# Three-block DMA transposes in a fused attention and feed-forward kernel, with one half batch turned by TensorE instead

## Chip, cores and metric

The kernel runs on one core of a Trainium2 chip. The metric is the device time of one execution in microseconds (us), given as the median of several executions. A profile is of one execution; its span is some 1.7 to 1.9 us shorter than the time of the same execution. All runs below are single-core, and all were classed as fast, with a granted TensorE clock of 0.99 to 1.00.

## What is computed

Windowed attention over 8 batches, 8 heads, 576 tokens and head size 64, then four matrix products over the 4608 tokens:

```python
def _attn_ref(q, k, v):                       # (8, 8, 576, 64) each
    scores = scale * np.matmul(q, k.transpose(0, 1, 3, 2))
    rel = pos[:, None] - pos[None, :]
    mask_plain = (rel >= 0) & (rel < 32)                         # heads 0 to 3
    mask_dil = (rel >= 0) & (rel < 128) & (rel % 4 == 0)         # heads 4 to 7
    # ... masked softmax ...
    return np.matmul(attn, v)

x = attn_out.transpose(0, 2, 1, 3).reshape(4608, 512)
out = (((x @ w1) * (x @ w2)) @ w3) @ w_out
```

The kernel forms w3 @ w_out once, so that each tile of 512 tokens needs 64 matmuls with w1 and w2 and 32 with the fused matrix.

## The kernel before

Attention is done in steps: for each batch b, first the dilated heads (`u = 1`), then the plain ones (`u = 0`), each in two halves `hf` of 288 tokens. A step ends with its normalised values in `xo`: 96 tokens on the partitions, and along the free dimension 2 pairs of heads, 3 blocks of 96 tokens, 2 heads, 64 channels. The feed-forward part needs channels on the partitions, in `XT` (four chunks of 128 channels, 4608 tokens), so every block of every pair is transposed. The dilated steps of batches 2 to 7 do it by DMA from SyncE, one DMA for each block and pair. All others use TensorE and a copy from PSUM.

```python
def to_channels(self, ps=ps_x, copy=None):
    if self.u and self.b > 1:
        for hp in range(2):
            for m in range(3):
                t0 = self.b * S + HALF * self.hf + 96 * m
                nc.sync.dma_start(
                    out=XT[:, 2 + hp, t0 : t0 + 96],
                    in_=self.xo[0:96, hp, 2 * m : 2 * m + 2, :].rearrange("p h d -> p (h d)"),
                    transpose=True,
                )
        return
    xv = ps[:, 0 : 2 * HALF].rearrange("p (h s t) -> p h s t", h=2, s=4)
    for hp in range(2):
        for m in range(3):
            # ... xo = 96 columns of xv
            nc.tensor.transpose(out=xo, in_=self.xo[0:96, hp, 2 * m : 2 * m + 2, :],
                                identity=ident[0:96, 0:96])
    # ... dst = the half's place in XT
    if copy is None:
        copy = nc.vector.tensor_copy if self.u == 0 and self.b > 1 else nc.scalar.copy
    copy(out=dst, in_=xv)
```

The phases of attention are spread between the matmuls of the feed-forward tiles; `after` is the room that a phase gets:

```python
# from segment(), for step i, with p1 the step before and p2 the one before that; tests on st left out
later(st.scores, after=1.0 if p2 is not None and p2.u == 0 else 1.6)
if p2 is not None and p2.u == 0:
    later(p2.to_channels)
    # ...
if p1 is not None:
    later(p1.values, after=1.6)
    if p1.u:
        behind(p1.to_channels)          # DMA: issued by SyncE once xo is there and its queue is free
    # ...
```

The consumer is the first feed-forward product, which takes chunks 2 and 3 (the dilated heads) first (shortened; from tile 1 on):

```python
for c in (2, 3, 0, 1):
    nc.tensor.matmul(out=ps, lhsT=w_sb[:, c, f * P : (f + 1) * P],
                     rhs=XT[:, c, t * TB : (t + 1) * TB], ...)
```

Token tile t ends at token 512(t+1), and batch b begins at token 576b. So tile 2 (to token 1535) needs the first of the three blocks (tokens 1440 to 1535) of batch 2's second half, and tile 3 needs 32 tokens of batch 3's second half. Tiles 4 to 7 need only the first half of their own batch, and tile 8 the rest of batch 7. "Landing" is used below for the time from the issue of a DMA to the arrival of its data.

The softmax here doesn't subtract the row's maximum and nothing guards it: scores larger than these inputs give would overflow.

Of the kernel before, what the change touches and what calls it, by code (L numbers as in the profile page):

```python
# [19 lines left out]
S = 576  # L20
D = 64
ROWS = 18
HALF = 288
# [13 lines left out]
def kernel(  # L37
# [11 lines left out]
    nc = tc.nc  # L49
# [34 lines left out]
    XT = const.tile([P, DCH, n_tok], BF16, name="XT")  # L84
# [171 lines left out]
    class Step:  # L256
        def __init__(self, n, b, u, hf):
            self.b, self.u, self.hf = b, u, hf
            self.et = ets[n % NET]
            self.xo = {}  # L260

        def score_matmuls(self, heads, bank_of, start):
# [101 lines left out]
            self.normalize(ov, self.xo.rearrange("p h j d -> p (h j) d"), 4, 3)()  # L364

        def to_channels(self, ps=ps_x, copy=None):
            if self.u and self.b > 1:
                for hp in range(2):
                    for m in range(3):
                        t0 = self.b * S + HALF * self.hf + 96 * m  # L370
                        nc.sync.dma_start(  # L371
                            out=XT[:, 2 + hp, t0 : t0 + 96],
                            in_=self.xo[0:96, hp, 2 * m : 2 * m + 2, :].rearrange("p h d -> p (h d)"),
                            transpose=True,
                        )
                return
            xv = ps[:, 0 : 2 * HALF].rearrange("p (h s t) -> p h s t", h=2, s=4)
            for hp in range(2):
                for m in range(3):
                    if self.u == 0:  # L380
                        xo = xv[:, hp, :, 24 * m : 24 * m + 24]
                    else:
                        xo = xv[:, hp].rearrange("p s t -> p (s t)")[:, 96 * m : 96 * m + 96]
                    nc.tensor.transpose(  # L384
                        out=xo,
                        in_=self.xo[0:96, hp, 2 * m : 2 * m + 2, :],
                        identity=ident[0:96, 0:96],
                    )
            dst = XT[:, 2 * self.u : 2 * self.u + 2, self.b * S : (self.b + 1) * S]
            if self.u == 0:  # L390
                t0 = 72 * self.hf
                dst = dst.rearrange("p h (s t) -> p h s t", s=4)[:, :, :, t0 : t0 + 72]
            else:
                t0 = HALF * self.hf
                dst = dst[:, :, t0 : t0 + HALF].rearrange("p h (s t) -> p h s t", s=4)
# [3 lines that stand above are left out]
# [19 lines left out]
    def later(f, *args, after=1.0):  # L418

        phases.append([lambda: f(*args)])  # L420
        room.append(after)

    def behind(f, *args):

        phases[-1].append(lambda: f(*args))
# [64 lines left out]
    def segment(lo, hi):  # L490

        for i in range(lo, hi + 2):
            st = steps[i] if i < hi else None
            p1 = steps[i - 1] if lo <= i - 1 < hi else None
            p2 = steps[i - 2] if lo <= i - 2 else None
            at, b = i % 4, i // 4
            more = 4 * (b + 1) < hi and st is not None
            if st is not None:
                later(st.scores, after=1.0 if p2 is not None and p2.u == 0 else 1.6)
            if p2 is not None and p2.u == 0:  # L500
                later(p2.to_channels)
                done_at[i - 2] = len(phases)
            if p1 is not None:
                later(p1.values, after=1.6)
                if p1.u:
                    behind(p1.to_channels)
            if st is not None:
                if at == 0:
                    behind(transpose_qk, b, 0, 1)
                if at == 1:  # L510
                    if more:
                        behind(transpose_qk, b + 1, 1, 0)
                if at == 2:
                    behind(prefetch, b + 2)
                if at == 2 and more:
                    behind(transpose_qk, b + 1, 1, 1)
                if at == 3 and more:
                    behind(transpose_qk, b + 1, 0, 0)

    second_batch()  # L520
    segment(8, 4 * B)


# [193 lines left out]
```

## Time and profile before

| | before |
|---|---|
| time, median (range) | 259.9 us (259.73 to 259.92, 3 runs) |
| span of the profiled run | 258.3 us |
| TensorE busy | 248.8 us, 96% |
| VectorE, ScalarE busy | 154.8 us, 110.6 us |
| DMA transposes, issue on SyncE | 72, median 1.228 us |
| DMA transpose, issue to landing | 2.2 / 3.3 / 9.3 us (least, median, most) |

The lines of the page, of TensorE's waits, of the chain of waits around 80 us and of the transposes' own view are shown and read in the prediction below. In a line of the timeline the columns are start, duration, engine, source line, operation, output <- inputs, shape and count; brackets at the end hold the idle time of the engine just before, and what ended it.

### The profile page before, as it was taken

The page shows a single profiled execution, that of the slowest core. Times are in us where ns is not written, and L with a number is a line of the kernel's source. Part 1 is how long each engine was busy: PE and PEld are TensorE (multiplying, and loading weights), DVE is VectorE, ACT ScalarE, POOL GpSimd, SP SyncE. Part 2 cuts the span into 40 slices and gives each one's busy share as a digit, 9 for nine tenths or more (in the row PEclk, how much of TensorE's full clock was granted, in tenths as well). Part 3 has the DMA queues.
Part 4 walks back from the last instruction along what each step waited for, and adds up shares of the span by engine and source line. Part 5 has one row for each costly group of instructions (what it writes and reads, how often), then busy time and mean ns, then how long its engine had stood idle before and what let it go on. Part 6 is the DMA issues. An engine that isn't in the chain of part 4 may idle for free.

```text
span 258.3 us, 5698 instructions
## 1 busy us (share of the span) xinstructions
PE 248.8 (96%) x2312; PEld 124.0 (48%) x2312; DVE 154.8 (60%) x326; ACT 110.6 (43%) x160; POOL 57.8 (22%) x84
## 2 busy tenths in 40 slices
PE   7789999999999989999999999999999999999994
PEld 3454455645444444554555454545544544444442
DVE  6675346867997657848875777578736623412420
ACT  1443356555554434344445544444454224334332
POOL 8962235537261114113211500000000000000000
PEclk9999999999999999999999999999999999999999
DMA  6999999999999989974998591212132131023013
GB/s 108 151 183 208 207 210 201 189 198 213 247 187 174 180 202 110 161 140 117 113 158 168 100 139 49 91 24 56 52 88 51 27 97 71 0 58 105 3 39 124
DMA packets 61177, 32.27 MB, mean 125 GB/s; under 512 B 47200, under 2 KB 51552, under 8 KB 61152
## 3 DMA queue, kind: packets, MB, share of 16 engines
q0 software_dynamic: 46160, 20.70, 66.6%
q1 hardware_dynamic: 14992, 11.22, 16.0%
q8 instruction: 18, 0.29, 0.5%
q14 instruction: 7, 0.06, 0.1%
HBM read 41.39 MB, written 9.44 MB: 197 GB/s over the span
## 4 chain that ended last, share of the span: by engine, by line
PE 70%; DMA 18%; DVE 4%; POOL 4%; issue 1%; SPq 1%; ACT 1%; POOLq 0%
PE f L528 40%; PE f L584 22%; DMA qn<-in_q_dram 11%; DMA XT<-xo 4%; PE ps_a L317 3%; DMA w_sb<-in_moe_w_dram 3%; PE ps_a L275 3%; PE ps_x L384 1%; DVE xo L328 1%; SPq L371 1%; POOL vd L140 1%; DVE kt L240 1%; PE f L614 1%; POOL w_sb L151 1%; POOL vp L131 1%
## 5 line engine op out<-in xcount | busy, mean ns | idle before, releaser
L528 PE MATMUL f<-XT,w_sb 128*128 128x512 bf16 x560 | 128.7, 379 | 1.4 <-DMA XT<-xo 1.4
L528 PEld LDWEIGHTS <-w_sb 128*128 128x128 bf16 x576 | 53.3, 98 | 62.0 <-issue 1.9
L559 DVE TENSOR_TENSOR gt<-f,asb 128x512 bf16<-128x512 f32 x70 | 48.0, 687 | 38.7 <-PE f L528 37.8
L558 ACT CAST asb<-f 128x512 bf16<-128x512 f32 x70 | 41.0, 586 | 66.1 <-PE f L528 63.6
L584 PE MATMUL f<-wf_sb,gt 128*128 128x512 bf16 (+1 forms) x296 | 67.3, 373 | 0.0
L591 ACT COPY osb<-f 128x512 f32<-128x512 f32 (+1 forms) x37 | 21.2, 574 | 47.5 <-PE f L584 47.2
L584 PEld LDWEIGHTS <-gt 128*128 128x128 bf16 x296 | 27.1, 98 | 27.9 <-DVE gt L559 0.5
L305 ACT ACTIVATE et<-ps_a 128x1152 bf16<-128x1152 f32 x28 | 31.7, 1134 | 8.2 <-PE ps_a L275 8.2
L140 POOL DMA_DIRECT2D vd<-in_v_dram x32 | 21.2, 669 | 41.7 <-PE ps_a L317 31.2
L328 DVE TENSOR_TENSOR xo<-ps_a,rcp 96x768 bf16<-96x768 f32 x28 | 26.7, 953 | 1.1
L247 DVE STREAM_TRANSPOSE qt<-qn 128x160 uint32<-128x160 uint32 (+1 forms) x64 | 19.6, 423 | 2.7 <-DMA qn<-in_q_dram 2.7
L306 DVE TENSOR_TENSOR et<-et,mask_di 128x1152 bf16<-128x1152 bf16 x14 | 10.6, 756 | 14.6 <-ACT et L305 14.6
L317 PEld LDWEIGHTS <-et 128*128 128x128 bf16 x384 | 15.8, 98 | 7.2 <-ACT et L295 0.6
L306 DVE TENSOR_TENSOR et<-et,mask_pl 128x1152 bf16<-128x1152 bf16 x14 | 10.6, 758 | 13.6 <-ACT et L305 13.5
L275 PEld LDWEIGHTS <-kt 32*128 32x128 bf16 x768 | 10.7, 93 | 15.6 <-issue 11.8
L614 PE MATMUL f<-wo_sb,w3T 128*128 128x512 bf16 x64 | 16.0, 379 | 0.1
L325 DVE RECIPROCAL rcp<-ps_a 96x12 f32<-96x12 f32 x28 | 6.2, 221 | 10.9 <-PE ps_a L317 10.8
L275 PE MATMUL ps_a<-qt,kt 32*128 32x96 bf16 x672 | 12.4, 202 | 0.3 <-DVE kt L247 0.2
L116 POOL DMA_DIRECT2D kn<-in_k_dram x10 | 6.4, 643 | 22.0 <-DVE kt L240 17.9
L116 POOL DMA_DIRECT2D qn<-in_q_dram x10 | 6.6, 662 | 18.5 <-DVE qt L247 14.8
L240 DVE STREAM_TRANSPOSE kt<-kn 128x576 uint32<-128x576 uint32 x8 | 10.0, 1245 | 0.9 <-DMA kn<-in_k_dram 0.9
L606 ACT COPY w3T<-f 128x1024 bf16<-128x1024 bf16 x7 | 7.1, 1012 | 6.8 <-PE f L600 6.8
(60 smaller groups left out, 137.7 us busy)
## 6 DMA issues: line engine op xcount, KB each, us to landing
qn<-in_q_dram POOLq DMA_DIRECT2D x6, 576.0 KB, 10.7
kn<-in_k_dram POOLq DMA_DIRECT2D x6, 576.0 KB, 10.4
w3n<-in_moe_w_dram POOLq DMA_DIRECT2D x4, 512.0 KB, 16.3
vp<-in_v_dram POOLq DMA_DIRECT2D x5, 384.0 KB, 7.9
out_dram<-osb SPq DMA_DIRECT2D x7, 256.0 KB, 2.3
out_dram<-osb SPq DMA_DIRECT2D x8, 224.0 KB, 2.5
out_dram<-osb SPq DMA_DIRECT2D x8, 192.0 KB, 4.1
out_dram<-osb SPq DMA_DIRECT2D x8, 160.0 KB, 3.8
```

The source lines that it names most:

```text
L140: nc.gpsimd.dma_start(out=vds[b % 2][p0 : p0 + n, 4 * m : 4 * m + 4, 16 : 16 + 2 * D], in_=bass.AP(tensor=x.tensor, offset=x.offset + (4 * ...
L247: nc.vector.transpose(out=bass.AP(tensor=o.tensor, offset=o.offset + at, ap=[o.ap[0], [1, n], [9, 16], [step, 2]],), in_=t[:, a0 : a0 + 4 ...
L275: nc.tensor.matmul(out=bank_of(h)[:, c0 : c0 + 96], lhsT=kt[prt, 96 * m : 96 * m + P, c], rhs=rhs, start=(start and c == 0), stop=(c == 1 ...
L305: nc.scalar.activation(out=ev, in_=ps_a[:, :, 0:HALF], func=ACT.Exp, scale=scale)
L306: nc.vector.tensor_tensor(out=ev, in0=ev, in1=mk.unsqueeze(1).to_broadcast([P, 4, HALF]), op=AL.mult)
L317: nc.tensor.matmul(out=out, lhsT=self.et[:, c0 : c0 + P], rhs=rhs, start=True, stop=True)
L328: nc.vector.tensor_tensor(out=xo[0:96].rearrange("p (n k) d -> p n k d", n=n), in0=ov[0:96, :, :, x0 : x0 + D], in1=rcp[0:96].unsqueeze(3) ...
L528: nc.tensor.matmul(out=ps, lhsT=w_sb[:, c, f * P : (f + 1) * P], rhs=XT[:, c, t * TB : (t + 1) * TB], start=(c == 2), stop=(c == 1),)
L558: nc.scalar.copy(out=a_sb, in_=ps)
L559: nc.vector.tensor_tensor(out=gts[t][:, f], in0=pss[1], in1=a_sb, op=AL.mult)
L584: nc.tensor.matmul(out=y, lhsT=gts[t][:, f, tb * P : (tb + 1) * P], rhs=wf_sb[:, f, c0 : c0 + n], start=(f == 0), stop=(f == KFF - 1),)
L591: nc.scalar.copy(out=o_sb[:, c0 : c0 + n], in_=y)
```

## The change

The intent is fewer DMAs: one takes the three blocks of a pair of heads at once, so a half needs two instead of six. Batch 2's second half, whose transposes came late, goes to TensorE. The diff in full:

```diff
--- before.py
+++ after.py
@@ -257,6 +257,8 @@
         def __init__(self, n, b, u, hf):
             self.b, self.u, self.hf = b, u, hf
             self.et = ets[n % NET]
+
+            self.by_dma = u == 1 and b > 1 and (b, hf) != (2, 1)
             self.xo = {}
 
         def score_matmuls(self, heads, bank_of, start):
@@ -364,15 +366,14 @@
             self.normalize(ov, self.xo.rearrange("p h j d -> p (h j) d"), 4, 3)()
 
         def to_channels(self, ps=ps_x, copy=None):
-            if self.u and self.b > 1:
+            if self.by_dma:
                 for hp in range(2):
-                    for m in range(3):
-                        t0 = self.b * S + HALF * self.hf + 96 * m
-                        nc.sync.dma_start(
-                            out=XT[:, 2 + hp, t0 : t0 + 96],
-                            in_=self.xo[0:96, hp, 2 * m : 2 * m + 2, :].rearrange("p h d -> p (h d)"),
-                            transpose=True,
-                        )
+                    t0 = self.b * S + HALF * self.hf
+                    nc.sync.dma_start(
+                        out=XT[:, 2 + hp, t0 : t0 + HALF].rearrange("p (m t) -> p m t", m=3),
+                        in_=self.xo[0:96, hp].rearrange("p (m h) d -> p m (h d)", m=3),
+                        transpose=True,
+                    )
                 return
             xv = ps[:, 0 : 2 * HALF].rearrange("p (h s t) -> p h s t", h=2, s=4)
             for hp in range(2):
@@ -496,13 +497,13 @@
             at, b = i % 4, i // 4
             more = 4 * (b + 1) < hi and st is not None
             if st is not None:
-                later(st.scores, after=1.0 if p2 is not None and p2.u == 0 else 1.6)
-            if p2 is not None and p2.u == 0:
+                later(st.scores, after=1.0 if p2 is not None and not p2.by_dma else 1.6)
+            if p2 is not None and not p2.by_dma:
                 later(p2.to_channels)
                 done_at[i - 2] = len(phases)
             if p1 is not None:
                 later(p1.values, after=1.6)
-                if p1.u:
+                if p1.by_dma:
                     behind(p1.to_channels)
             if st is not None:
                 if at == 0:
```

## The prediction

> **What bounds the kernel now.** I read the page from the top. The busy shares say TensorE; the slices say where it isn't busy.
>
> ```profile
> span 258.3 us, 5698 instructions
> PE 248.8 (96%) x2312; PEld 124.0 (48%) x2312; DVE 154.8 (60%) x326; ACT 110.6 (43%) x160; POOL 57.8 (22%) x84
> ...
> PE   7789999999999989999999999999999999999994
> ```
>
> TensorE is busy for 248.8 of 258.3 us, and its clock row on the page is 9 in every slice, so no throttle is in play. Only 258.3 - 248.8 = 9.5 us can be won by removing waits of any kind. The next view is the list of who waited for whom, for TensorE alone:
>
> ```profile
> PE ps_x L179 <- DVE mp L185: 1.5, 1, 1.5
> PE f L528 <- DMA XT<-xo: 1.4, 1, 1.4
> PE ps_s L275 <- DVE kt L247: 1.1, 1, 1.1
> PE ps_s L275 <- DVE rcp L325: 0.3, 1, 0.3
> ```
>
> The columns are total us, number of waits, longest. The 1.5 and 1.1 us lie in the start-up. In the same list confined to 60 to 210 us, the stretch in which the changed code runs, the second line is the only one left: one wait of 1.4 us, for a DMA transpose. The chain of waits between 79 and 93 us shows how it comes about, and the timeline of TensorE shows its size:
>
> ```profile
> 78.14 0.96 DVE xo L328
> 79.10 0.31 SPq L371
> 79.42 0.04 issue
> 79.46 1.23 SPq L371
> 80.69 0.04 issue
> 80.73 1.23 SPq L371
> 81.97 0.04 issue
> 82.01 9.28 DMA XT<-xo
> ```
>
> ```profile
> 89.55 0.38 PE L528 MATMUL f<-XT,w_sb 128*128 128x512 bf16 x1
> 91.33 0.81 PE L528 MATMUL f<-XT,w_sb 128*128 128x512 bf16 x3 [1.41 <-DMA XT<-xo]
> ```
>
> SyncE issues the blocks one after another. The second half of the third batch (b = 2, tokens 1440 to 1727) starts its six at 78.3 us. The fourth is the first block of the second head pair (tokens 1440 to 1535, channel chunk 3); it is issued at 82.01 and lands 9.28 us later, at 91.29. Token tile 2 (tokens 1024 to 1535) starts at 89.55: its first matmul reads chunk 2 and runs, its second reads chunk 3 and waits until 91.33. All other halves land in time, as no later wait shows.
>
> One more line, from the view of the source line with the transposes:
>
> ```profile
> L371 SPq DMA_TRANSPOSE XT<-xo x72: 1092/1228/2495, 70.0 to 205.6; - x72
> ...
>   PE f L528: 1.4, 1
> ...
> DMA to landing us min/median/max: 2.2/3.3/9.3
> ```
>
> There are 72 issues of 1.228 us each, about 88 us of SyncE, but SyncE holds nobody up except in that one place. Landing depends on the other traffic: 7.0 to 9.3 us in the windows from 70 to 86 us, where the view by stretches gives a DMA share of 1.58 to 1.75 (prefetch of batch 3), and 2.3 us after 175 us, where the share is 0.17 to 0.27.
>
> **What the Trainium skill says.** "DMA: Bandwidth & Descriptors", section "DMA Transpose (X-bar)": two-byte types only, partitions a multiple of 16, issued by SyncE or ScalarE. The trace agrees (all on SyncE, 96 partitions, bf16), and the new form keeps to it. The same page, "Anatomy of one DMA": the fixed cost of a DMA is about 2.0 us, mostly the receipt of the last write. The fastest transposes here land in 2.2 us with 24 KB (96 x 128 x 2 bytes), which agrees: three blocks in one DMA should pay that fixed part once. Its "Rules for kernel authors" say to coalesce many small transfers. "TensorE: Matmul & The Clock Gate", "Part 4: PE-mode transpose": about 275 ns for a 128x128 transpose in context, and the result lies in PSUM and needs a copy. The trace has records of 205 ns for 96x96, but they overlap: the six of a half hold TensorE's queue for only 0.26 us (80.74 to the next group at 81.00; 0.25 at 86.33 and at 105.38), so I use 0.26.
>
> **The change, part by part.**
>
> (1) Third batch, second half, to TensorE. It removes the 1.41 us wait: xo is ready at 79.1, the transposes come one phase after the next scores, about 81 us, then ScalarE copies for 0.64 us (the same copy, six times before, mean 639 ns), possibly behind an exponential of 1.14 us. XT is then written by about 84 us, against 89.55 when it is needed: 5 us to spare. Added on TensorE's path: one group of six, 0.26 us. The copy is off the path: ScalarE idles 0.8 to 1.9 us before each eviction between 80 and 90 us. Sum: -1.41 + 0.26 = -1.15 us.
>
> (2) Three blocks in one DMA, for the 11 remaining halves: 66 issues become 22. SyncE is relieved, by 66 x 1.23 = 81 us less 22 times the cost of a new issue. If an issue were a fixed cost, 22 x 1.23 = 27 us would be left; if it goes by the block, nothing is saved. In both cases TensorE gains 0, as it waits for none of these 11 halves now. The stores behind them on SyncE leave earlier, but the end of the kernel is the last output tile (final eviction at 254.57 us), long after the last transpose at 205.6.
>
> (3) Pacing. The new TensorE transposition is a phase of its own, so batch 2's phases are placed a little closer together: by my count of the spacing weights, 17.2 units instead of 16.8 over the same 23 points, 2%. This moves instructions by fractions of a us. I put 0 on it, with up to 0.3 us either way.
>
> Total: 259.9 - 1.15 = 258.75, told as 258.7 us, that is 0.45% less.
>
> **The rivals.**
>
> (a) The wait moves to the next tile. Batch 3's second half must give tokens 2016 to 2047 to tile 3, which starts at 115.7 us. Its xo is ready at 97.1 us; SyncE issues now from 101.65, and the landing takes 3.2 to 5.4 us. A DMA of three blocks is only done as a whole, so the first block now waits for the third. If an issue costs three times as much (3.7 us), the second pair's DMA starts at 97.1 + 3.7 = 101 if SyncE is free then, or 105.4 if not, and with 3.7 of issue and the 5.4 it lands at 110 to 114.5. That is 1 to 6 us before the need: hidden, but not by far in the worst case. A stall of 1 to 2 us here would eat the gain and give 259.9 to 260.8. I give it 10%. From batch 4 on, tile t needs only the first half of batch t at once, which has 17 us or more.
>
> (b) The three-block form is slow, because its source and destination are strided in the middle dimension or because it makes worse descriptors. Then prefetches of q, k and v behind it suffer. They have some room (TensorE waits for no load after 40 us), and it takes a landing of above 14 us instead of 4 before TensorE notices. I give 4% to a loss of over 2% this way (5 us or more would need several stalls).
>
> (c) The gain is larger, because shorter transposition traffic also frees VectorE and prefetch. Against it: from 100 to 250 us the view by stretches has TensorE busy 10.00 of every 10 us. There is nothing to gain there; 0.2 us at most.
>
> (d) The new copy on ScalarE delays an exponential or an eviction, and TensorE then waits for a PSUM bank (there are three to go round) or for the one tile that all transposes of xo pass through. ScalarE is 43% busy in these stretches; I allow 0.3 us.
>
> **Range and chances.** The centre is the sum, 258.7. Below: all of the wait gone and (c), 258.0. Above: half of rival (a), 259.9. A gain of 2% would need 254.7 us, more than half of all the idle time that TensorE has, most of it at the start and the end: 1%. Slower by 2% needs 265.1 us: 2%.
>
> **What would show each step right or wrong.** Right: in the changed kernel's list of TensorE's waits the line for XT<-xo is gone, 22 DMA transposes are left, the group of TensorE transposes of xo has 126 instead of 120 instructions and ScalarE one more copy into XT, and TensorE's busy time is up by about 0.3 us while the span is down by 1.1. Step 2 is judged by the mean issue of a transpose on SyncE: 1.2 us if fixed, 3.7 if by the block; I lean to something between, about 1.6. The prediction is wrong if a wait for XT<-xo appears at the start of tile 3 or later, if landings of the long transposes exceed 10 us, or if TensorE waits for the copy into XT around 82 to 88 us.

## The result

| | before | changed |
|---|---|---|
| time, median (range) | 259.81 us (259.59 to 259.92, 4 runs) | 258.18 us (258.02 to 258.56, 4 runs) |
| ratio, 95% interval | | 0.994 (0.9923 to 0.9958) |
| span of the profiled run | 258.3 us | 256.4 us |

A ratio is the mean time of one kernel's fast runs over the mean of the other's fast runs of the same rounds, so it is not quite the ratio of the medians. The time fell by 1.63 us and lies within the predicted range.

The page of the changed kernel, and its list of TensorE's waits (total us, times, longest):

```profile
span 256.4 us, 5585 instructions
PE 246.9 (96%) x2281; PEld 124.7 (49%) x2318; DVE 154.7 (60%) x326; ACT 111.2 (43%) x161; POOL 57.7 (23%) x84
```

```profile
PE ps_x L179 <- DVE mp L185: 1.5, 1, 1.5
PE ps_s L277 <- DVE kt L247: 0.8, 1, 0.8
PE f L585 <- issue: 0.8, 5, 0.2
PE f L529 <- issue: 0.5, 3, 0.2
...
```

The wait for `XT<-xo` is gone. The two lines with "issue" are holes in the records: there are 2318 weight loads (PEld) but 2281 matmuls, so 37 matmul records are missing, and each hole in these two lines reads as some 0.16 us of idleness. TensorE's busy time in this profile is too low for the same reason. A second profile of the changed kernel has all 2318 records and 249.2 us, 0.4 more than before. The start of tile 2 in the timeline of TensorE:

```profile
88.71 1.03 PE L585 MATMUL f<-wf_sb,gt 128*128 128x512 bf16 x4
89.57 1.03 PE L529 MATMUL f<-XT,w_sb 128*128 128x512 bf16 x4
```

Where four matmuls were torn apart (one at 89.55, three at 91.33), they now run as one group. And the view of the tile `xo`, where a line has the least, median and largest duration in ns:

```profile
L385 PEld LDWEIGHTS <-xo x126: 95/97/100, 16.3 to 207.8; 96*128 96x128 bf16 x126
...
L372 SPq DMA_TRANSPOSE XT<-xo x22: 1172/1240/2315, 69.8 to 195.9; - x22
...
DMA to landing us min/median/max: 2.3/3.6/10.3
```

There are 22 DMA transposes and 126 on TensorE. A three-block DMA takes 1.240 us to issue where one block took 1.228. In quiet stretches it lands in 2.3 us, one block in 2.2.

**A measure without scatter.** Executions of one kernel differ by 0.3 to 3.4 us, which is as much as the effect. Up to about 60 us TensorE runs beside the first loads, and what happens there differs from execution to execution: 16 identical warm-up matmuls took between 4.92 and 6.52 us in the 14 profiles. After that TensorE hardly stops. So I measure, in each profile, the stretch from TensorE's last group of transposes for batch 1 to the last eviction of an output tile. Its two ends before the change and, in the second fence, after:

```profile
61.31 0.42 PE L384 MATMUL ps_x<-ident,xo 96*128 96x96 bf16 x6
254.57 0.37 ACT L591 COPY osb<-f 128x256 f32<-128x256 f32 x1 [0.50 <-PE f L584]
```

```profile
61.08 0.42 PE L385 MATMUL ps_x<-ident,xo 96*128 96x96 bf16 x6
253.03 0.37 ACT L592 COPY osb<-f 128x256 f32<-128x256 f32 x1 [0.50 <-PE f L585]
```

That is 193.26 us before and 191.95 after: -1.31. The rest of the difference of the spans (-1.90) is -0.23 before the stretch and -0.36 after it. This is the table for all kernels; "tail" is the time from the start of the last eviction to the end of the span.

| kernel | late DMA at tile 2 | TensorE groups against before | stretch, us | tail, us |
|---|---|---|---|---|
| before | yes | 0 | 193.26 | 3.73 |
| changed, two profiles | no | +1 | 191.95, 191.95 | 3.37, 3.30 |
| tensor_only, two profiles | no | +1 | 191.96, 191.96 | 3.75, 3.72 |
| wide_only, two profiles | no | 0 | 191.69, 191.70 | 3.75, 3.72 |
| wide_one | no | 0 | 191.69 | 3.43 |
| block_order | no | 0 | 191.70 | 3.70 |
| no_v3 (wrong result) | no | 0 | 191.70 | 3.70 |
| all_tensor | no | +12 | 194.81 | 3.84 |
| wide_b1_half | no | 0 (-1 ahead of the stretch) | 191.70 | 3.70 |
| wide_b1, two profiles | no | 0 (-2 ahead of the stretch) | 191.69, 193.23 | 3.49, 3.44 |

With one exception, told below, the stretch repeats to 0.02 us: 193.26 with the wait, 191.70 without it, and 0.26 more for each added group. The kernel before was profiled only once, so the 193.26 is of one execution. That the wait comes back in the others is seen from the times alone: by the medians, every kernel below that has no wait and adds at most one group is 0.8 to 1.9 us faster than the kernel before in the same rounds.

### The profile page after: what moved, and what is told of

Its sections match the earlier page's. It is cut to its first block, busy times and chain, and to the rows that moved or that the text cites. A ratio compares the mean times of both kernels' runs of the same rounds, so it can differ in the third digit from the quotient of the medians.

```text
span 256.4 us, 5585 instructions
## 1 busy us (share of the span) xinstructions
PE 246.9 (96%) x2281; PEld 124.7 (49%) x2318; DVE 154.7 (60%) x326; ACT 111.2 (43%) x161; POOL 57.7 (23%) x84
## 4 chain that ended last, share of the span: by engine, by line
PE 90%; DVE 3%; DMA 2%; issue 2%; ACT 1%; POOL 0%; POOLq 0%; ACTq 0%
PE f L529 45%; PE f L585 24%; PE f L615 5%; PE ps_a L319 4%; PE ps_a L277 4%; DMA kn<-in_k_dram 2%; PE ps_x L385 2%; PE ps_b L529 1%; PE f L601 1%; PE ps_s L277 1%; PE ps_s L293 1%; PE ps_x L179 1%; DVE xo L330 1%; DVE kt L240 0%; DVE gt L560 0%
## 5 line engine op out<-in xcount | busy, mean ns | idle before, releaser
L529 PE MATMUL f<-XT,w_sb 128*128 128x512 bf16 x537 | 127.0, 379 | 1.5 <-issue 0.5
L585 PE MATMUL f<-wf_sb,gt 128*128 128x512 bf16 (+1 forms) x288 | 66.0, 373 | 1.0 <-issue 0.8
L277 PE MATMUL ps_a<-qt,kt 32*128 32x96 bf16 x672 | 12.4, 202 | 0.1
L247 DVE STREAM_TRANSPOSE kt<-kn 128x160 uint32<-128x160 uint32 (+1 forms) x32 | 9.7, 416 | 1.6 <-DMA kn<-in_k_dram 1.5
L297 ACT ACTIVATE et<-ps_s 128x576 bf16<-128x576 f32 x8 | 5.2, 651 | 11.9 <-PE ps_s L277 11.6
```

Source lines behind the costliest of these rows:

```text
L247: nc.vector.transpose(out=bass.AP(tensor=o.tensor, offset=o.offset + at, ap=[o.ap[0], [1, n], [9, 16], [step, 2]],), in_=t[:, a0 : a0 + 4 ...
L277: nc.tensor.matmul(out=bank_of(h)[:, c0 : c0 + 96], lhsT=kt[prt, 96 * m : 96 * m + P, c], rhs=rhs, start=(start and c == 0), stop=(c == 1 ...
L585: nc.tensor.matmul(out=y, lhsT=gts[t][:, f, tb * P : (tb + 1) * P], rhs=wf_sb[:, f, c0 : c0 + n], start=(f == 0), stop=(f == KFF - 1),)
```

## The experiments

Twelve runs. Where one differs from the kernel before or the changed one, the edit is shown short.

### Each part alone: tensor_only, wide_only, and the changed kernel again

tensor_only is the changed kernel with the six single-block DMAs put back in the branch:

```diff
             if self.by_dma:
                 for hp in range(2):
-                    # one DMA of three blocks
+                    for m in range(3):      # one DMA a block, as before
```

> Only the third batch's second half goes to TensorE; the other 11 halves keep DMA transposes of one block (66 issues). Theory A (the whole gain is the one wait at the start of token tile 2; the three-block form is worth nothing to TensorE): TensorE's wait for XT<-xo gone, ratio to before 0.994 to 0.996 (start-to-start the wait costs 1.56 us, the added group 0.26), within 0.2% of the changed kernel. Rival B (shorter transposition traffic or earlier stores give part of the gain): ratio 0.997 or above, and the changed kernel clearly faster than this one.

Measured: 258.98 us (258.25 to 259.88), ratio 0.9963 (0.9940 to 0.9986), just outside what theory A named. The wait is gone, and the stretch is 191.96.

wide_only keeps the three-block form and moves nothing to TensorE:

```diff
-            self.by_dma = u == 1 and b > 1 and (b, hf) != (2, 1)
+            self.by_dma = u == 1 and b > 1
```

> Only the three-block form, for all 12 halves, the third batch's second half too; no added TensorE group. Theory C (the late landing came from SyncE's serial issues: the xo in question is ready at 74.2 us, but its fourth block is issued only at 82.0, behind the six issues of the half before and three of its own): its two DMAs are issued at about 74.3 and 75.5, land by 86 even at 10.3 us each, before the need at 89.8; no wait left, TensorE groups of xo as before (120), ratio 0.993 to 0.9945, that is 0.1% faster than the changed kernel. Rival D (the landing under prefetch traffic is what counts, and a DMA done only as a whole makes it longer): the wait stays, at 0.5 us or more, ratio 0.997 or above.

Measured: 257.89 us (257.79 to 258.29), ratio 0.9927 (0.9910 to 0.9944). There is no wait either, with the 120 TensorE transposes of before. SyncE's timeline, the start of tile 2, and the landing of the late half's two DMAs:

```profile
69.75 7.03 SPq L372 DMA_TRANSPOSE XT<-xo  x4
```

```profile
89.29 1.03 PE L529 MATMUL f<-XT,w_sb 128*128 128x512 bf16 x4
```

```profile
DMA to landing us min/median/max: 9.1/9.2/9.3
```

The late half's two DMAs are issued at 74.0 and 75.2 us and land 9.3 and 9.1 us later, the second at 84.3, five us before the need. Theory C holds and rival D falls: the landing is as long as before, but the issue is seven us earlier.

The changed kernel again, on the same chip:

> The changed kernel once more, for a second profile and times of the same rounds as its parts. Theory: ratio 0.994 plus or minus 0.001, no wait for XT<-xo; what its first profile had beyond 1.3 us (0.23 us up to 61 us, 0.36 us after the last eviction) is run to run scatter and need not come back.

Measured: 258.08 us (257.49 to 258.72), ratio 0.9935 (0.9915 to 0.9955), stretch 191.95. The lead up to 61 us didn't come back (61.45 now, 61.31 before the change). The shorter tail did (3.30), which I had not expected.

So each part by itself removes the wait. Done together, the second one done is idle: with the DMAs wide, moving the half to TensorE only adds its group.

tensor_only's time was 0.9 us worse than the changed kernel's, with the same stretch, so it was run again:

> The TensorE part alone once more, since its times (258.98 us) were worse than the changed kernel's (258.08), while the two traces are equal from TensorE's transposes at 61 us on (191.96 and 191.95 us to the last eviction). Theory A: the difference is scatter of the start; this time ratio 0.993 to 0.996, within 0.15% of the changed kernel, and the stretch from the last transposes of the second batch to the last eviction is again 191.9 to 192.0 us. Rival B (the three-block form is worth 0.3% by itself): ratio 0.997 again, and the profile again starts late.

Measured: 258.44 us (258.19 to 258.89), ratio 0.9962 (0.9940 to 0.9983), stretch again 191.96. The ratio lies just outside what theory A named and short of what rival B named, and it is again some 0.3% above the changed kernel's (0.9935), where theory A allowed 0.15%. The intervals of the two overlap. The traces show where some 0.4 us of it lies, and it isn't in the transposes: both its profiles have a tail of 3.7 us, and both of the changed kernel 3.3 to 3.4. In the tail SyncE waits for the last store: the list of SyncE's waits has 1.6 us for it in both profiles of tensor_only and 1.1 us in both of the changed kernel. The form of the DMAs doesn't decide it: wide_only, with all of them wide, has a tail of 3.7 us, and wide_one, with 66 single ones, 3.4. Why the tail follows the program is open. For the other 0.5 us of the first comparison the start is a candidate, but one profile per run can't show it: tensor_only's first profile had batch 1's last transposes at 62.39 us, its second at 60.72.

### The order of the blocks: block_order

The kernel before, with the two loops exchanged, so that the block that tile 2 needs is second of six in place of fourth:

```diff
-                for hp in range(2):
-                    for m in range(3):
+                for m in range(3):
+                    for hp in range(2):
```

> The kernel before with one change: blocks outer, pairs inner, so that the first block of both pairs is issued first. All 72 issues stay. Theory C: the block that tile 2 waits for is issued second of its half instead of fourth, at 79.5 us, 2.5 us earlier, and lands at 86.5 to 88.8; the wait is gone, ratio 0.993 to 0.995. Rival D (landing set by traffic that ends at 91 us, whatever the time of issue): the wait stays near 1.4 us, ratio 0.999 to 1.001.

Measured: 258.17 us (257.80 to 258.73), ratio 0.9938 (0.9918 to 0.9957), stretch 191.70. SyncE's timeline and tile 2:

```profile
69.39 15.97 SPq L371 DMA_TRANSPOSE XT<-xo  x12
```

```profile
88.94 1.03 PE L528 MATMUL f<-XT,w_sb 128*128 128x512 bf16 x4
```

SyncE is as busy as before with its twelve issues in a row. The needed block is issued at 79.0, lands 6.7 us later at 85.7, a little earlier than expected, and there is no wait. By the stretch, an exchange of two lines gains 0.25 us more than the whole change; by the times the two can't be told apart.

### Only the half that stands in the way: wide_one

The kernel before, with the three-block form for batch 2's first half alone:

```diff
+            # by_dma: u == 1 and b > 1, the halves that go by DMA before
+            if self.by_dma and (self.b, self.hf) == (2, 0):
+                # two DMAs of three blocks, return
             if self.by_dma:
                 # six DMAs of one block, as before
```

> The kernel before, with the three-block form in one place only: the third batch's first half, the one that stands on SyncE ahead of the half that came late. Theory C (SyncE's backlog made it late): the late half's six single blocks are issued from about 74 us instead of 78.3, its fourth by 78 and landed by 86, the wait at tile 2 is gone, the stretch from the second batch's last transposes to the last eviction is 191.7 us as where all halves are wide, ratio 0.992 to 0.9955. Rival D (traffic alone sets the landing): wait above 0.7 us, the stretch above 192.4.

Measured: 257.77 us (257.38 to 258.45), ratio 0.9932 (0.9909 to 0.9956), stretch 191.69. SyncE's timeline:

```profile
69.17 2.57 SPq L372 DMA_TRANSPOSE XT<-xo  x2
73.42 7.91 SPq L382 DMA_TRANSPOSE XT<-xo  x6
```

The late half itself is unchanged, with its six single blocks, which landed in 8.2 to 9.8 us. Because the half ahead of it takes 2.57 us of SyncE and not 8.3, it begins at 73.42 instead of 78.3. This shows directly that the backlog on SyncE made the DMA late.

### The traffic: no_v3

The kernel before without the loads of v for batch 3. The result is wrong (relative error 0.50).

```diff
             load_qk(b)
+            if b == 3:
+                return
             load_vd(b)
             load_vp(b)
```

> A wrong result on purpose: the kernel before without the two loads of v for the fourth batch (b = 3), that is 352 + 384 KB less traffic issued between 73 and 77 us. Issue times on SyncE stay as before. If traffic of the prefetch makes the landings of 7 to 9 us (theory G): landings of the second half's six fall to 3 to 5 us, the fourth lands by 87, the wait at tile 2 is gone, ratio 0.993 to 0.995. If it is the queue of transposes itself or the loads of q and k (rival H): landings stay at 7 to 9 us and the wait stays above 0.7 us, ratio 0.997 or above.

Measured: 258.43 us (257.95 to 259.09), ratio 0.9959 (0.9931 to 0.9987), stretch 191.70, no wait. The ratio lies between what the two theories named, and neither is right as I put it. The expectation also names the wrong loads: batch 3's v is issued from 59.2 to 63.3 us in the kernel before, and has landed by 75.7 (the source line that loads `vp` for batches 3 to 7 runs five times, first at 61.9). The v issued between 73 and 77 us is batch 4's, and no_v3 still loads it (its load `vp`, issued at 75.0, lands in 7.3 us in place of 12.1). So the run takes 736 KB out of the traffic ahead of the late half, and the loads behind it land sooner. The landings of the late half's six are 3.8, 7.8, 6.7, 5.7, 4.7 and 6.1 us, neither all short nor as long as before. The second to the fifth of them land within 0.7 us of each other, at 88.1 to 88.8. In the kernel before, the fourth to sixth land at 91.3 to 92.1, and the view of DMA issues between 78 and 82 us has this next to them (KB each, us to landing):

```profile
qn<-in_q_dram POOLq DMA_DIRECT2D x1, 576.0 KB, 10.7
```

That load of q, for batch 5, is issued at 80.6 us and lands at 91.3, with the fourth transpose (91.29). Without batch 3's v it took 6.4 us. The transposes issued from 82 us on landed when that load did or later; the one issued at 80.7, while the load itself was being issued, landed at 87.8. The traffic is the other half of the cause: take away either the backlog or one batch's v (736 of the 1888 KB that are loaded for a batch), and the data comes in time. That the load of q itself holds the transposes back is only a coincidence of times so far: I have not tried to take it away.

### All halves on TensorE: all_tensor

```diff
-            self.by_dma = u == 1 and b > 1 and (b, hf) != (2, 1)
+            self.by_dma = False
```

> All 12 halves that took DMA transposes go to TensorE (the 22 DMAs gone, 11 more groups of six than in the changed kernel). Theory: a group costs TensorE 0.26 us and nothing else, so the stretch from the second batch's last transposes to the last eviction is 191.95 + 11 x 0.26 = 194.8 us, ratio 1.003 to 1.006 (before: 193.26). Rival E (the copy on ScalarE and the shared PSUM tile cost more than the group): above 195.5 us with new waits of TensorE. Rival F (transposes hide in gaps): below 193 us.

Measured: 261.35 us (260.86 to 261.89), ratio 1.0070 (1.0046 to 1.0093), stretch 194.81. From the changed kernel that is 2.86 us for 11 groups, or 0.26 each, the size used in the prediction. The ratio is a little above what I wrote (1.003 to 1.006), the stretch is as expected, and no wait for PSUM or ScalarE appeared. Rivals E and F fall.

### Going further: wide_only again, wide_b1_half, wide_b1

If wide DMAs are cheap, batch 1's dilated halves could use them too, each saving TensorE a group. wide_b1 does so for both halves, wide_b1_half for the first; batch 2 and later are as in wide_only.

```diff
-            self.by_dma = u == 1 and b > 1 and (b, hf) != (2, 1)
+            self.by_dma = u == 1 and b > 0                          # wide_b1
+            self.by_dma = u == 1 and b > 0 and (b, hf) != (1, 1)    # wide_b1_half
```

> Three-block DMAs for all 12 halves and for the second batch's two as well, which are turned by TensorE before and after. Theory: two groups fewer on TensorE, -0.52 us, if their XT lands before tile 1 at 63.5 us: issued at 47 to 53 us beside the end of the weight loads, with a landing of up to 10 us they do; ratio 0.990 to 0.992, no wait for XT<-xo. Rival D: landing beside the loads takes 12 us or more, TensorE waits at tile 1, ratio 0.994 or above.

Measured: 257.85 us median, but from 256.97 to 260.37, ratio 0.9960 (0.9917 to 1.0004), where 0.990 to 0.992 was expected. The gain that theory named is not seen in the ratio.

> The same kernel as wide_b1, to see its scatter again (256.97 to 260.37 us before). If the slow executions belong to it, two or more of six are above 258.3; if they were chance, none is, and the median is 257.0 to 257.4. The stretch from the second batch's last transposes to the last eviction is 191.7 us in any case, so a slow profile should show its loss before 61 us or at tile 1.

Measured: 257.64 us (257.26 to 259.28), ratio 0.9939 (0.9911 to 0.9966). Two of six are above 258.3, so by the rule set beforehand the scatter belongs to it; but the kernel before scattered by 2.0 and 1.6 us in the same two sessions, and the evidence of the times is weak. The profile caught one of the slow ones (259.28 us), and its loss is neither before 61 us nor at tile 1, as I had expected, but at 71 to 75 us. From the timelines of VectorE and of TensorE:

```profile
71.17 1.24 DVE L247 STREAM_TRANSPOSE qt<-qn 128x160 uint32<-128x160 uint32 x4 [1.67 <-DMA qn<-in_q_dram]
```

```profile
72.98 1.89 PE L529 MATMUL f<-XT,w_sb 128*128 128x512 bf16 x7 [0.79 <-DVE gt L560]
75.37 0.45 PE L277 MATMUL ps_a<-qt,kt 32*128 32x96 bf16 x24 [0.50 <-DVE xo L330]
```

The next batch's q comes late, VectorE stands still in front of it for 1.67 us, and TensorE waits for VectorE. That is the 1.53 us by which this profile's stretch (193.23) exceeds 191.70. The load in question took 10.9 us to land in the kernel before (10.5 to 11.0 in every profile that shows it and has no DMA transposes for batch 1), 14.1 and 15.5 in the two profiles of wide_b1. Transposes issued at 47 to 53 us, beside loads, go together with loads that land later.

> As wide_only, and the second batch's first half by DMA as well (one group of TensorE less), its second half on TensorE as before. Its two DMAs are issued at 47 to 48.4 us and land by 58, tile 1 needs them at 62.5. If the slow executions of wide_b1 (258.5 to 260.4 us beside 257.0) came from the second half's landing close to the need: none above 258.3 here, median 257.2 to 257.7, ratio 0.990 to 0.9925. If they come from transposes beside the weight loads at all, or from the start's own scatter: spread again above 2 us.

Measured: 258.03 us (257.45 to 259.86), ratio 0.9948 (0.9921 to 0.9975). The expected ratio (0.990 to 0.9925) was missed. Two of six are above 258.3 (258.33 and 259.86) and the spread is 2.4 us, so slow executions occur without DMA transposes of the second half. Only wide_b1_again's profile is of a slow one, so what made the others slow isn't shown. In this run's profile, of a fast execution, the load in question took 12.4 us. Neither variant is clearly better than wide_only:

> Three-block DMAs for all 12 halves, no half moved to TensorE, a second time, as the best candidate so far: ratio 0.992 to 0.9945, no wait for XT<-xo, the stretch 191.7 us again.

Measured: 258.22 us (258.05 to 259.25), ratio 0.9954 (0.9933 to 0.9975), just outside the expected ratio; stretch 191.70. By the stretch, wide_only, wide_one and block_order are each 0.26 us better than the changed kernel. By the times that isn't resolved: the intervals of all of them overlap that of the changed kernel, whose ratios were 0.994 and 0.9935. No version beat it beyond doubt.

One more attempt didn't build: a single DMA for one block of both pairs, from `xo` in its present layout. Its reason isn't shown here. In `xo` the two pairs lie 384 elements apart, while the three blocks of one pair lie side by side.

## Why the prediction was right, and where its steps were not

**The bound and the place** were right. TensorE bounds the kernel, and one wait at the start of tile 2 was all that this change could win; the stretch shows -1.56 us for it in every kernel without the wait and nothing beside it.

**The size of the wait** was low. I took 1.41 us, the idle time in brackets. The matmul ahead of the gap is recorded as 0.38 us long, but matmuls in a row start 0.216 us apart (12 of them take 2.59 us in the chain). Starts were 91.33 - 89.55 = 1.78 us apart in place of 0.22: the loss was 1.56 us, and that is what the stretch gives (193.26 - 191.70). The predicted -1.15 should have been -1.56 + 0.26 = -1.30; measured in the stretch, -1.31.

**The added group** cost 0.26 us as said: from the anchor to tile 2 it is 28.24 us before and 28.49 after.

**When xo is ready** was read wrongly, without harm. I took the VectorE product at 78.14 us, which the chain of waits puts ahead of the DMAs. Their own was one earlier (timeline of VectorE, kernel before):

```profile
73.27 0.95 DVE L328 TENSOR_TENSOR xo<-ps_a,rcp 96x768 bf16<-96x768 f32 x1
...
78.14 0.95 DVE L328 TENSOR_TENSOR xo<-ps_a,rcp 96x768 bf16<-96x768 f32 x1
```

Values with `vd`, the dilated heads, are multiplied at 67.7 and 72.1 us and with `vp` at 77.3, so the product at 73.27 is the dilated second half's, ready at 74.22, and the one at 78.14 belongs to the plain heads. (Lines of the timeline are left out between the two.) SyncE could begin that half only at 78.3, because the twelve issues stand in one row:

```profile
70.00 15.81 SPq L371 DMA_TRANSPOSE XT<-xo  x12
```

In the changed kernel TensorE therefore turned the half at 76.21 us, not at about 81, and XT was written by 77.3. More important, with the right time I would have seen that step (2), the wide form, also frees this half. The prediction gave all of the gain to step (1); wide_only shows that step (2) alone removes the wait, and without the added group. "SyncE holds nobody up except in that one place" was written, and not followed to its end. That the sum came out right all the same was luck: step (1) and step (2) remove the same wait, so crediting only one of them changed nothing in the total.

**Whose traffic it was.** The prediction calls the traffic from 70 to 86 us the prefetch of batch 3. The last of batch 3's loads had landed at 75.7 us; what was issued from 64.6 to 77 us is batch 4's q, k and v, and at 80.6 batch 5's q. The sum doesn't rest on it, but no_v3 was planned on this misreading.

**Step 2, the issue cost.** I leaned to 1.6 us between 1.2 and 3.7. It is 1.24, with three blocks as with one (1.23). SyncE's issues of transposes fall from 88 us to about 27.

**Rival (a)**, a wait at tile 3, stayed away with more room than I gave it: those DMAs are issued at 95.6 and 96.8 us and land by 102.7, against a need at 114.2. SyncE was free when xo was ready.

**Rival (b)**: one landing exceeded the 10 us that I named as a sign of being wrong (10.3 us, issued at 71.1), but it was there at 81.4 and needed at 89.6. Landing time alone says nothing without the time of need.

**Rivals (c) and (d)** and the pacing of step (3) left no trace: no wait for PSUM or for the copy into XT, and the stretch closes to 0.01 us without them.

**The rest of the total.** The median fell by 1.63 us. The stretch gives 1.31 of it. About 0.4 us is a shorter tail that both profiles of the changed kernel have and that the change doesn't explain. The scatter of the start is larger than what is left. So the comparison to make is 1.15 us predicted against 1.31 measured; that the whole 1.63 lies in the range says little about the steps. Why the tail differs between programs is open.

## What to carry to other kernels

When a transfer comes late, first ask when its data was ready and when it was issued: here nearly 8 us (74.2 to 82.0) passed in the issuing engine's own queue, and the order of the issues, fewer issues, or another engine for one piece each removed the wait. Look for the cheapest one, and don't pay for a second after the first has worked. To measure effects of under 1%, find a stretch of the trace that begins after the start-up and ends before the last stores: but for the slow execution of wide_b1_again it repeated to 0.02 us where whole executions scattered by 0.3 to 3.4 us.

## What the Trainium skill lacked or had wrong

- "DMA: Bandwidth & Descriptors", "DMA Transpose (X-bar)", has no issue cost for a DMA transpose between places in SBUF; the page's only sequencer costs of transposes stand in a comparison of trn3 with earlier chips, for tiles from HBM and for 8,192 tiles in SBUF, and none is for one DMA of a few blocks. Here one holds SyncE for 1.228 us with one block of 96 x 128 two-byte elements and 1.240 us with three (medians of 72 and 22), against 0.413 us for a plain store from the same queue.
- The same page's "Anatomy of one DMA" gives a fixed part of about 2.0 us, but for DMAs issued from GpSimd; it has no such fit for those from SyncE. Quiet landings of the transposes, which SyncE issues, are near it (2.2 us with one block, 2.3 with three). Under the prefetch of later batches the same DMAs took 7.0 to 9.3 us with one block (kernel before, issued at 70 to 85 us) and 9.1 to 11.7 with three (wide_only's two profiles and wide_one, issued at 69 to 76), and the page has no figure for small transfers behind large ones.
- "TensorE: Matmul & The Clock Gate", "Part 4: PE-mode transpose", gives about 275 ns for one transpose in context. Records here are 206 ns for 96 x 96, but a group of six holds TensorE for 0.26 us in all (11 added groups: 2.86 us), 43 ns for each; the page doesn't say that they overlap.
- No page that I read tells that a gap in a matmul stream is larger than the idle time shown: 1.41 us of idleness was 1.56 us lost.
